# Moving the first batch's second Fourier transform behind the first value products

## The chip, the cores and the metric

The kernel runs on one core of a Trainium2 chip. The metric is the device time of one execution in microseconds (us). Three runs of the kernel before took 630.52, 630.96 and 631.91 us; their median is 630.96 us.

The engines named below are PE (TensorE, matrix products), DVE (VectorE), ACT (ScalarE), POOL (GpSimd) and SP (SyncE, which here only issues transfers). Each executes its own instructions strictly in the order in which they were written; between engines there are semaphore waits.

## The reference

The program computes attention with capped scores (cap 30), then a token mixer by a Fourier transform with a feed-forward layer, then a gated layer. Cut to the parts that matter here:

```python
# attention, 2 batches x 12 heads, 448 tokens, 64 channels a head
scores = cap * np.tanh(scale * (q @ k.T) / cap)
attn = softmax(scores); x = attn @ v            # -> (2, 448, 768)
# Fourier mixing and layer norm
X = np.fft.fft(np.fft.fft(x, axis=1), axis=2)
u = x + np.real(X)
un = (u - mean(u)) / np.sqrt(var(u) + 1e-6)     # over the 768 channels
u = u + np.maximum(un @ w_ch1, 0.0) @ w_ch2     # then the gated layer
```

## The kernel before

Everything is kept transposed: channels on partitions, 448 tokens along the free axis. The heads go two by two, so there are 12 pairs, numbered 0 to 11; pairs 0 to 5 are the first batch, 6 to 11 the second. A hand-written software pipeline (`loop`, lines 608 to 682) runs over the pairs and is inside `tc.manual_schedule()`: each engine does its work in exactly the written order.

One turn n of the loop does, in the order of PE:

- `values(n - 1, (0, 1))`, line 568: the first half of the value products (tile `o`) of the pair before;
- `scores(n, 3)`, line 542: the last score block of this pair (tile `s_3`);
- `turn(n + 1)`, line 511: the transposes of the next pair's keys and queries (tile `tr`);
- `values(n - 1, (2, 3))` and `totals(n - 1)`, lines 568, 579 and 581: the second half of `o`, and the softmax's denominators (tile `den`);
- `scores(n + 1, step)` for steps 0, 1, 2: the next pair's scores (tiles `s_0`, `s_1`, `s_2`).

ACT turns scores into tanh (line 547) and then exponentials (line 551). DVE makes the low halves of keys and queries (line 520), the reciprocals of the denominators (line 588) and the product with them (line 592). POOL adds up exponentials (lines 556 and 560).

The first batch is complete after pair 5. What follows for it, the Fourier transform and the layer norm, is put into the gaps of the second batch's pairs. A table named `others` (lines 982 to 1011) says at which place of which turn each piece stands. The places are, in the order of a turn: "loads", "values" (behind the first value products), "transposes" (behind `turn` and the last tanh), "halves", "values23" (behind the second value products), "halves" (behind the first exponentials, in spite of its name), "take", "divide", "score0" to "score2" (behind each step of the next scores). The pieces of this change are:

- `f.second(c)` for c = 0, 2, 4, line 252: the second stage of the transform for channel blocks c and c+1, eight matmuls into one tile `st`;
- `f.add(c)`, lines 259 to 262: four DVE instructions that add a block of `st` to x, in tile `xT`;
- `n0.total`, lines 272 to 275: DVE sums u over channel blocks into `acc_m`; `n0.mean`, line 286: one matmul, tile `mu`; `n0.centre`, line 291: two DVE instructions d = u - mu; `n0.square`, line 298: two ACT instructions; `n0.square_total`: DVE sums again, into `acc_v`; then `n0.variance` (lines 307 to 309), `n0.deviation` (lines 314 and 316) and `n0.row` (line 323) in turn 11;
- `part("w2_", i, ...)`: steps of the conversion of a weight block from 8-byte to 4-byte floats: 0 size (ACT, line 704), 1 clamp (709), 2 shift (712), 3 top (715), 4 bottom (718), 5 upper (721, on DVE for i = 0), 6 lower (724). Steps 1 to 4 and 6 are DVE's.

PSUM's tiles `s_*`, `tr`, `st` and `mu` share three buffers of two banks (`big_ps`, line 112; 3 of them by line 940). A new tile waits until the readers of the buffer's last tile are done. `o` and `den` have one buffer each.

After turn 12 comes a long stretch of matrix products (feed-forward, gated layer, output) in which PE works nearly without a gap.

Of the kernel before, what the change touches and what calls it, by code (L numbers as in the profile page):

```python
# [93 lines left out]
def attention_mixers_kernel(ctx, tc, bounded, q, k, v, cap, w_ch1, w_ch2, w_in, g_ln, w_sg, b_sg, w_out,  # L94
# [839 lines left out]
    with ExitStack() as fctx:  # L934
# [8 lines left out]
        with ExitStack() as actx:  # L943
# [8 lines left out]
            if bounded:  # L952
                f, n0 = fourier(0, fp, t2sb, POOL_FOLDS[0]), layer_norm(0, fp)
                f1, n1 = fourier(1, fp, t2sb), layer_norm(1, fp)
                raws, pieces = {}, {}
                do = functools.partial
# [6 lines left out]
                def convert(*key):  # L963
                    name, i = key
                    how = dict(raw=raws[key], pieces=pieces.setdefault(key, []))
                    if name == "w1_":
                        w1.append(columns(w_ch1, i, name, hi_copy=vec.tensor_copy, **how))
                    else:
                        w2.append(rows(w_ch2, i, name, hi_copy=None if i else vec.tensor_copy, **how))

                def part(name, i, *steps):

                    def go():
                        if (name, i) not in pieces:
                            convert(name, i)
                        for step in steps:
                            pieces[name, i][step]()

                    return go
# [18 lines left out]
                    (8, "transposes"): [do(f.first, 1, 3)],  # L998
                    (8, "halves"): [do(f.keep_first, 1), do(f.keep_first, 3), part("w1_", 3, 5, 6), do(f.reverse, 0),
                                    do(f.reverse, 1), part("w2_", 0, 1, 2, 3)],  # L1000
                    (8, "take"): [do(f.second, 0), do(f.add, 0), do(f.add, 1)], (8, "score2"): [part("w2_", 0, 4)],
                    (9, "transposes"): [do(f.second, 2)],
                    (9, "halves"): [do(f.add, 2), do(f.add, 3), part("w2_", 0, 5, 6)],
                    (9, "divide"): [do(f.second, 4)],
                    (9, "score1"): [do(f.add, 4), do(f.add, 5)], (9, "score2"): [n0.total, part("w2_", 1, 0, 1, 2)],
                    (10, "loads"): [do(get, "w2_", 2)],
                    (10, "transposes"): [n0.mean], (10, "halves"): [n0.centre],
                    (10, "take"): [n0.square, n0.square_total],
                    (11, "loads"): [do(f1.table, kind) for kind in (0, 2, 1, 3)],
                    (11, "transposes"): [n0.variance, n0.deviation, None], (11, "values23"): [n0.row],  # L1010
                }
# [2 lines left out]
            else:  # L1014
                load, prepare, score, flip, values = attention(ap, mix)
# [264 lines left out]
```

## Time and profile before

| | us |
|---|---|
| median of 3 runs | 630.96 (630.52 to 631.91) |
| the profiled execution | 632.45 |
| span of the profiled execution | 630.7 |
| PE busy | 615.2 (98%) |
| DVE busy | 494.0 (78%) |
| ACT busy | 271.2 (43%) |
| POOL busy | 105.3 (17%) |

The profiled execution is one run under the profiler; its span goes from the first to the last recorded instruction, and 1.75 us lie around it. A timeline row gives the start in us from the span's beginning, the duration, the engine, the line, the operation and its tiles, and in brackets how long the engine was idle before it and which instruction ended that. Equal instructions in succession are one row with a count; a matmul on 32-bit floats has two records, so eight of them show as x16. Matmuls are pipelined: a row's duration holds the tail of its last one, and the difference of two starts is the time that PE needs.

The stretch of the change is from 94 to 135 us: the scores of pair 9 begin at 97.26 us, those of pair 10 at 112.82 us, those of pair 11 at 124.28 us.

### The profile page before, as it was taken

To read this page: it belongs to the slowest core of one execution; us is meant where nothing else is said; L and a number is where in the kernel's file an instruction comes from. 1 tells how busy PE (TensorE), PEld (TensorE's weight loads), DVE (VectorE), ACT (ScalarE), POOL (GpSimd) and SP (SyncE) were. 2 spreads that over 40 slices of the span, in tenths; PEclk is the share of its full clock that TensorE was granted. 3 is DMA by queue.
4 is the path that set the end of the run, shared out by engine and by line. 5 is a ranking of instruction groups with operands and counts; after the bars stand their busy time and mean duration, and the time that the engine had idled before them with its cause. 6 is when DMAs were issued, how large, how long until landed. Compare 5 with 4: busy or idle time off the path is not lost.

```text
span 630.7 us, 8755 instructions
## 1 busy us (share of the span) xinstructions
PE 615.2 (98%) x3378; PEld 529.7 (84%) x3378; DVE 494.0 (78%) x727; ACT 271.2 (43%) x371; POOL 105.3 (17%) x153
## 2 busy tenths in 40 slices
PE   7999999899999999999999999999999999999996
PEld 5555576559888999999999999999999999989985
DVE  1789999999985688989966893788389879897551
ACT  3999865672312244334503440442135245453221
POOL 1877795353000000000000000000000000100000
PEclk9999999999999999999999999999999999999998
DMA  6746523300400146444530522245035304100123
GB/s 160 194 103 161 164 67 79 133 1 1 151 1 16 51 150 207 153 151 151 168 133 8 193 101 101 76 128 195 3 107 184 111 2 150 51 1 1 30 73 78
DMA packets 70034, 62.84 MB, mean 100 GB/s; under 512 B 36256, under 2 KB 63712, under 8 KB 69984
## 3 DMA queue, kind: packets, MB, share of 16 engines
q1 hardware_dynamic: 69056, 61.97, 32.2%
q8 instruction: 28, 0.46, 0.3%
q10 hardware_dynamic: 928, 0.23, 0.2%
q14 instruction: 22, 0.18, 0.1%
HBM read 59.44 MB, written 2.75 MB: 99 GB/s over the span
## 4 chain that ended last, share of the span: by engine, by line
PE 91%; DVE 6%; ACT 1%; DMA 1%; issue 0%; POOLq 0%; POOL 0%; ACTq 0%; DVEq 0%
PE h L143 27%; PE c L143 27%; PE o L568 5%; PE v L143 5%; PE out L143 5%; PE u L143 5%; PE s L542 5%; PE sg L143 2%; PE st L231 2%; PE den L579 1%; PE den L581 1%; PE tr L511 1%; PE st L252 1%; DVE r L588 1%; PE idle L155 1%; PE xt L907 1%
## 5 line engine op out<-in xcount | busy, mean ns | idle before, releaser
L143 PE MATMUL h<-un,w 128*128 128x448 f32 x864 | 175.0, 363 | 0.5 <-DVE un L335 0.5
L143 PE MATMUL c<-h,w 128*128 128x448 f32 x864 | 174.8, 363 | 0.0
L143 PEld LDWEIGHTS h<-un,w 128*128 128x128 f32 x864 | 161.7, 187 | 12.7 <-DVE un L335 0.8
L143 PEld LDWEIGHTS c<-h,w 128*128 128x128 f32 x864 | 161.9, 188 | 11.5 <-issue 0.4
L767 DVE TENSOR_TENSOR xT<-xT,c 128x448 f32<-128x448 f32 x60 | 36.9, 616 | 35.7 <-PE c L143 35.7
L1225 POOL CAST x<-x 128x384 fp32r<-128x384 f32 x2 | 1.3, 672 | 324.8 <-ACT x L134 324.3
L547 ACT ACTIVATE e<-s,tanh_scale 128x896 f32<-128x896 f32 (+1 forms) x48 | 41.0, 933 | 16.1 <-PE s L542 15.9
L568 PE MATMUL o<-e,v 128*64 128x448 f32 x192 | 41.1, 551 | 0.0
L556 POOL TENSOR_TENSOR t<-e 128x224 f32<-128x224 f32 x48 | 39.6, 856 | 2.9 <-POOL mix L531 2.0
L560 POOL TENSOR_TENSOR t<-t,e 128x224 f32<-128x224 f32 x48 | 39.7, 858 | 0.0
L551 ACT ACTIVATE e<-e,cap_pos 128x1792 f32<-128x1792 f32 (+1 forms) x24 | 37.7, 1622 | 0.0
L758 ACT ACTIVATE h<-h 128x448 fp32r<-128x448 f32 x40 | 21.7, 543 | 27.4 <-DVE h L759 17.5
L588 DVE RECIPROCAL r<-den 128x448 f32<-128x448 f32 x11 | 32.4, 2947 | 1.1 <-PE den L581 1.0
L143 PE MATMUL out<-gated,wo 128*128 128x448 f32 x144 | 30.8, 367 | 0.0
L143 PEld LDWEIGHTS v<-wv,x 128*128 128x128 f32 x252 | 29.7, 188 | 0.1
L143 PE MATMUL v<-wv,x 128*128 128x256 f32 x252 | 29.7, 279 | 0.0
L143 PE MATMUL u<-x,wu 128*128 128x448 f32 x144 | 29.1, 362 | 0.0
L542 PE MATMUL s<-qT,kT 64*128 64x448 f32 x216 | 26.4, 379 | 2.3 <-DVE qT L520 1.2
L542 PEld LDWEIGHTS s<-qT,kT 64*128 64x128 f32 x216 | 19.2, 184 | 11.1 <-ACT e L551 4.2
L143 PEld LDWEIGHTS u<-x,wu 128*128 128x128 f32 x144 | 26.9, 188 | 1.8
L143 PEld LDWEIGHTS out<-gated,wo 128*128 128x128 f32 x144 | 26.4, 188 | 2.0 <-ACT gated L134 0.2
L568 PEld LDWEIGHTS o<-e,v 128*64 128x64 f32 x192 | 11.8, 136 | 17.7 <-issue 16.2
(383 smaller groups left out, 891.5 us busy)
## 6 DMA issues: line engine op xcount, KB each, us to landing
k<-in_k SPq DMA_DIRECT2D x24, 112.0 KB, 2.7
out<-res SPq DMA_DIRECT2D x12, 224.0 KB, 2.5
q<-in_q SPq DMA_DIRECT2D x22, 112.0 KB, 2.7
t<-dft_channels SPq DMA_DIRECT2D x8, 291.0 KB, 4.9
v<-in_v SPq DMA_DIRECT2D x24, 96.0 KB, 2.3
w_0raw<-in_moe_w_ch SPq DMA_DIRECT2D x2, 768.0 KB, 5.1
w_1raw<-in_moe_w_ch SPq DMA_DIRECT2D x2, 768.0 KB, 5.8
w_2raw<-in_moe_w_ch SPq DMA_DIRECT2D x2, 768.0 KB, 4.7
```

The lines of the kernel that those rows point to most:

```text
L143: pe.matmul(ps, lhs(i, a), rhs(i, b), start=start and m == 0, stop=stop and m == last)
L155: pe.matmul(ps[:, 0:2 * P], idle[:, 0:P], idle, start=True, stop=True)
L231: pe.matmul(ps[:HS, m * 256:m * 256 + NE], fold[:, i, m * HS:(m + 1) * HS], tab[:, i, :], start=i == 0, stop=i == 2)
L542: pe.matmul(ps[:, i, :S], t[lo:hi, x, at:at + P], qT[lo:hi, y, :], start=m == 0, stop=m == 2)
L547: act.activation(es[n][:, 2 * step:2 * step + nr], sums.pop((n, step))[:, :nr, :S], AF.Tanh, scale=tanh_scale)
L551: act.activation(part, part, AF.Exp, scale=cap_pos)
L556: pool.tensor_tensor(t[:, j, q], es[n][:, j, q], es[n][:, 2 + j, q], op=ALU.add)
L560: pool.tensor_tensor(ts[n][:, j, q], ts[n][:, j, q], es[n][:, 4 + j, q], op=ALU.add)
L568: pe.matmul(os[n][halfs[j], :S], vts[n % 3][:, j, i], es[n][:, 2 * i + j if i < 3 else 6], start=i == 0, stop=i == 3)
L588: vec.reciprocal(r, den[:, :S])
L758: act.activation(h[:, 0], ps[:, i, :S], AF.Relu)
L767: vec.tensor_tensor(u[:, c, :], u[:, c, :], ps[:, :S], op=ALU.add)
```

## The change

The three `f.second` calls of the first batch leave their places, and so do their adds, the mean's sum, the mean and several conversions:

- `f.second(0)` stood before the scores of pair 9 ((8, "take")) and now stands behind the first value products of pair 8 ((9, "values")). Its adds come behind the reciprocal of pair 7 on DVE.
- `f.second(4)` stood before the scores of pair 10 ((9, "divide")) and now stands behind the first value products of pair 9 ((10, "values")). Its adds and `n0.total` go to turn 10 with it.
- `n0.mean` stood behind the transposes of turn 10 and now stands behind the second value products of pair 9 ((10, "values23")).
- Steps 5 and 6 of weight block 0 (DVE) move from turn 9 to turn 10, ahead of `n0.centre`; step 4 moves from behind the scores of pair 9 to turn 9's "halves".
- Steps 0, 1, 2 of weight block 1 (ACT, DVE, DVE) move from the end of turn 9 to the end of turn 10, behind the squares on ACT.

```diff
-                    (8, "take"): [do(f.second, 0), do(f.add, 0), do(f.add, 1)], (8, "score2"): [part("w2_", 0, 4)],
-                    (9, "transposes"): [do(f.second, 2)],
-                    (9, "halves"): [do(f.add, 2), do(f.add, 3), part("w2_", 0, 5, 6)],
-                    (9, "divide"): [do(f.second, 4)],
-                    (9, "score1"): [do(f.add, 4), do(f.add, 5)], (9, "score2"): [n0.total, part("w2_", 1, 0, 1, 2)],
+                    (9, "values"): [do(f.second, 0)],
+                    (9, "transposes"): [do(f.add, 0), do(f.add, 1), do(f.second, 2)],
+                    (9, "halves"): [part("w2_", 0, 4), do(f.add, 2), do(f.add, 3)],
                     (10, "loads"): [do(get, "w2_", 2)],
-                    (10, "transposes"): [n0.mean], (10, "halves"): [n0.centre],
+                    (10, "values"): [do(f.second, 4), do(f.add, 4), do(f.add, 5), n0.total],
+                    (10, "values23"): [n0.mean],
+                    (10, "halves"): [part("w2_", 0, 5, 6), n0.centre],
                     (10, "take"): [n0.square, n0.square_total],
+                    (10, "score2"): [part("w2_", 1, 0, 1, 2)],
```

On PE, around the scores of pair 10 (`s`), before: `st_0_4` is the last second unit, `o` the value products of pair 9, `tr` the transposes for pair 11, `mu` the mean.

```order
L252 MATMUL st_0_4_1227<-t2sb,back_1_1094 128x226 x2
L542 MATMUL s_0_1236<-qT_1189,kT_1188 128x448 x6
L542 MATMUL s_1_1243<-qT_1189,kT_1188 128x448 x6
L542 MATMUL s_2_1258<-qT_1189,kT_1188 128x448 x6
L568 MATMUL o_1285<-e_1070,v_148 64x448 x4
L542 MATMUL s_3_1292<-qT_1189,mix_134 128x448 x3
L511 MATMUL tr_1297<-ident,k_1143 128x112 x4
L511 MATMUL tr_1297<-ident,q_1146 128x112 x4
L286 MATMUL mu_1307<-acc_m_1267,mean_w 128x448
L568 MATMUL o_1285<-e_1070,v_148 64x448 x4
```

The same place of PE in the changed kernel:

```order
L542 MATMUL s_2_1239<-qT_1188,kT_1187 128x448 x6
L568 MATMUL o_1256<-e_1070,v_148 64x448 x4
L252 MATMUL st_0_4_1261<-t2sb,back_0_1092 128x226 x2
L252 MATMUL st_0_4_1261<-t2sb,back_1_1094 128x226 x2
L252 MATMUL st_0_4_1261<-t2sb,back_0_1092 128x226 x2
L252 MATMUL st_0_4_1261<-t2sb,back_1_1094 128x226 x2
L542 MATMUL s_3_1285<-qT_1188,mix_134 128x448 x3
L511 MATMUL tr_1290<-ident,k_1125 128x112 x4
L511 MATMUL tr_1290<-ident,q_1128 128x112 x4
L568 MATMUL o_1256<-e_1070,v_148 64x448 x4
L286 MATMUL mu_1313<-acc_m_1280,mean_w 128x448
```

The last second unit has passed three score steps and half of the value products, and the mean has passed the other half.

On DVE, from the last add of channel block 5 to the centring, before: `half` and `acc_m` are the mean's sum, `w_1cvt` a conversion of block 1, `kT` and `qT` the low halves of pair 11, `d` the centred tokens.

```order
L262 TENSOR_TENSOR xT_105<-xT_105,st_0_4_1227 128x223
L272 TENSOR_TENSOR half_1265<-xT_105 128x3x448
L274 TENSOR_TENSOR acc_m_1267<-half_1265 128x448
L275 TENSOR_TENSOR acc_m_1267<-acc_m_1267,half_1265 128x448
L709 TENSOR_SCALAR w_1cvt<-w_1cvt 128x768
L712 TENSOR_SCALAR w_1cvt<-w_1cvt 128x768
L520 TENSOR_TENSOR kT_1309<-tr_1297,kT_1309 128x448
L520 TENSOR_TENSOR qT_1310<-tr_1297,qT_1310 128x448
L291 TENSOR_TENSOR d_0_1333<-xT_105,mu_1307 128x1344
L291 TENSOR_TENSOR d_1_1335<-xT_105,mu_1307 128x1344
```

The same stretch of DVE in the changed kernel:

```order
L262 TENSOR_TENSOR xT_105<-xT_105,st_0_4_1261 128x223
L272 TENSOR_TENSOR half_1278<-xT_105 128x3x448
L274 TENSOR_TENSOR acc_m_1280<-half_1278 128x448
L275 TENSOR_TENSOR acc_m_1280<-acc_m_1280,half_1278 128x448
L520 TENSOR_TENSOR kT_1300<-tr_1290,kT_1300 128x448
L520 TENSOR_TENSOR qT_1301<-tr_1290,qT_1301 128x448
L721 CAST w_0_1011<-w_0cvt 128x768
L724 TENSOR_TENSOR w_0_1011<-w_0cvt,w_0_1011 128x768
L291 TENSOR_TENSOR d_0_1328<-xT_105,mu_1313 128x1344
L291 TENSOR_TENSOR d_1_1330<-xT_105,mu_1313 128x1344
```

Two conversion steps left the place ahead of `kT`, and two others, of block 0, came in between `qT` and the centring.

On PE, the next pair's scores in the changed kernel, with what they wait for (PE_49 is PE's own semaphore, DVE_49 is DVE's):

```order
L542 MATMUL s_1_1349<-qT_1301,kT_1300 128x448 [waits PE_49]
L542 MATMUL s_1_1349<-qT_1301,kT_1300 128x448 x5
L542 MATMUL s_2_1356<-qT_1301,kT_1300 128x448 [waits DVE_49,PE_49]
L542 MATMUL s_2_1356<-qT_1301,kT_1300 128x448 x5
L568 MATMUL o_1380<-e_1193,v_149 64x448 [waits DMAHW4_49,Activation_49]
L568 MATMUL o_1380<-e_1193,v_149 64x448 [waits DMAHW7_49]
L568 MATMUL o_1380<-e_1193,v_149 64x448 x2
L542 MATMUL s_3_1387<-qT_1301,mix_135 128x448 [waits Activation_49,Pool_49]
```

In both kernels `s_2` of pair 11 takes the PSUM buffer of `mu`, so it waits for the second centring instruction; `s_3` takes the buffer of `s_0`, so it waits for that tile's tanh.

## Rows read from the trace of the kernel before

**Rows 1.** Busy time and share of the span of each engine, from the page.
```profile
PE 615.2 (98%) x3378; PEld 529.7 (84%) x3378; DVE 494.0 (78%) x727; ACT 271.2 (43%) x371; POOL 105.3 (17%) x153
```

**Rows 2.** PE's waits, whole span: total us, times, longest us.
```profile
PE mu L286 <- DVE acc_m L275: 1.7, 2, 1.2
...
PE s L542 <- ACT e L547: 1.1, 2, 0.6
PE st L252 <- ACT pq L235: 0.9, 1, 0.9
```

**Rows 3.** PE timeline, pairs 9 to 11: start, us, instructions, idle time before.
```profile
99.30 0.89 PE L542 MATMUL s<-qT,kT 64*128 64x448 f32 x6 [0.56 <-ACT e L547]
...
109.57 3.32 PE L252 MATMUL st<-t2sb,back 113*128 113x226 f32 x16
...
120.20 0.99 PE L286 MATMUL mu<-acc_m,mean_w 128*128 128x448 f32 x2 [1.25 <-DVE acc_m L275]
121.12 1.72 PE L568 MATMUL o<-e,v 128*64 128x448 f32 x8
...
124.28 2.09 PE L542 MATMUL s<-qT,kT 64*128 64x448 f32 x18
...
127.95 0.88 PE L542 MATMUL s<-qT,mix 128*128 128x448 f32 x3
128.68 1.48 PE L155 MATMUL var<-ident 128*128 128x256 bf16 x12
```

**Rows 4.** Chain of waits in order of time: start, us, what.
```profile
93.33 0.75 PE den L581 x4
94.08 3.25 PE st L252 x16
...
100.19 1.65 PE o L568 x8
101.84 0.81 PE s L542 x3
102.65 0.77 PE tr L511 x8
...
124.35 2.02 PE s L542 x18
```

**Rows 5.** DVE timeline: conversions, first add, mean's sum, halves, centring; columns as PE's.
```profile
108.91 0.92 DVE L721 CAST w<-w_0cvt 128x768 fp32r<-128x768 f32 x1
109.87 1.29 DVE L724 TENSOR_TENSOR w<-w_0cvt,w 128x768 fp32r<-128x768 f32 x1
...
114.68 0.38 DVE L259 TENSOR_TENSOR xT<-xT,st 128x225 f32<-128x225 f32 x1
...
117.18 1.56 DVE L272 TENSOR_TENSOR half<-xT 128x1344 f32<-128x1344 f32 x1
...
121.04 0.62 DVE L520 TENSOR_TENSOR kT<-tr,kT 128x448 fp32r<-128x448 f32 x1
...
122.10 3.01 DVE L291 TENSOR_TENSOR d<-xT,mu 128x1344 f32<-128x1344 f32 x2
...
158.44 0.95 DVE L724 TENSOR_TENSOR w<-w_1cvt,w 128x768 fp32r<-128x768 f32 x1
```

**Rows 6.** ACT timeline: conversion's first step, squares, tanh of pair 11.
```profile
108.64 0.94 ACT L704 ACTIVATE w_1cvt<-w_1raw 128x768 f32<-128x768 f32 x1
...
123.68 2.80 ACT L298 ACTIVATE sq<-d 128x1344 f32<-128x1344 f32 x2 [0.23 <-DVE d L291]
126.38 3.31 ACT L547 ACTIVATE e<-s,tanh_scale 128x896 f32<-128x896 f32 x4
```

**Rows 7.** PE timeline, the first matmuls after the start, on idle data.
```profile
3.29 5.30 PE L155 MATMUL idle<-ident 128*128 128x256 bf16 x24 [3.29 <-POOL ident masks.py:199]
```

**Rows 8.** Stretches at the end: length, busy us by engine (PE first), PEclk, DMA.
```profile
624.50:625.00 0.50, 0.16 (x2) 0.00 (x0) 0.00 (x0) 0.26 (x1) 0.00 (x0) 1.00 0.14 33
...
626.50:627.00 0.50, 0.00 (x0) 0.00 (x0) 0.00 (x0) 0.00 (x0) 0.00 (x0) 0.80 0.18 47
```

## The prediction

> **What bounds the kernel now.** I read the page's busy shares first: PE is busy 98% of the span [rows 1], and no other engine is above 78%. PE's work is the same in both kernels, instruction by instruction, so the time can change only by the time in which PE stands still, or by PE's rate. PE's list of waits over the whole span comes next [rows 2]. Few are left, and three lie in the stretch of the change: the scores of pairs 9 and 10 each wait for a tanh, 0.56 us and 0.55 us (1.1 us in two, one of them shown [rows 2, 3]), and the mean waits 1.25 us for its sum [rows 3]. Together 2.36 us: that is all that the change could win here. Then I read the timelines of PE, DVE and ACT from 94 to 135 us to see what each instruction would wait for in its new place, and the chain of waits for PE's durations between gaps [rows 4]. The reader is to see in the DVE rows that the mean's wait ends with a DVE chain (adds, sum), and that the next tile on PE's way depends on the centring that follows it [rows 5].
>
> **The change part by part.** PE's durations are those of the chain [rows 4]: a pair's scores 2.02 us, half of the value products 1.65, a second unit 3.25, the last score block 0.81, the transposes 0.77, the denominators twice 0.75.
>
> *First second unit behind the value products.* Both kernels have finished the denominators at 93.33 + 0.75 = 94.08 us. From there the new order on PE is scores 2.02, values 1.65, unit 3.25, last scores 0.81, transposes 0.77, unit 3.25, values 1.65, denominators 1.50, scores 2.02, values 1.65: 18.57 us, so the last unit begins at 112.65. Both waits for tanh go, 1.11 us, since `s_2` no longer has to take the buffer of `s_0` just written. What each of these pieces needs is there: keys, queries and exponentials are made at least 1 us earlier. I cost this part at -1.11 us.
>
> *Last second unit and its adds.* It begins at 112.65 instead of 109.57 [rows 3]. Before, its result lay waiting, since DVE still had two conversions and a reciprocal to do and began the adds at 114.68 [rows 5]. Now DVE has nothing left by then and stands idle until the unit has ended: 112.65 + 3.32 (the unit's row [rows 3]) + 0.05 = 116.0. The cover that the conversions gave is gone, and the adds come 1.3 us later.
>
> *Sum and mean.* From the first add to the mean on PE it took 120.20 - 114.68 = 5.52 us, eight adds and three sums with nothing between [rows 3, 5]. So the mean begins at 116.0 + 5.5 = 121.5. PE gets there at 112.65 + 3.25 + 0.81 + 0.77 + 1.65 = 119.1. It waits 2.4 us instead of 1.25, although half of the value products now fills the time ahead of it.
>
> *Conversions ahead of the centring.* The sum ends at 121.4. Behind it on DVE stand the low halves of pair 11, 122.10 - 121.04 = 1.06 us, then the two conversion steps of block 0, 0.96 us (start to start) and 1.29, and then the two centring instructions, 3.01 [rows 5]: 121.4 + 1.06 + 2.25 + 3.01 = 127.7. Before, the centring ended at 122.10 + 3.01 = 125.1. On PE come the mean 0.92 (120.20 to 121.12 [rows 3]), denominators 1.50, and two of three score steps, two thirds of 2.02: 121.5 + 0.92 + 1.50 + 1.35 = 125.3. Then `s_2` of pair 11 needs the mean's buffer, which the centring holds until 127.7. That is a new wait of 2.4 us; before, PE came at 124.28 + 1.35 = 125.6, after the buffer was free, and so had none. Behind `s_2` on PE stand the value products and everything else of the turn. The conversions' 2.25 us is measured beside POOL's additions; the same step took 0.95 us instead of 1.29 where POOL was idle [rows 5]. In the new place POOL begins its additions of pair 10 within these steps, so I take the larger value; two steps that are both 0.35 us faster would take 0.7 us from the sum.
>
> By the Trainium skill (SBUF — State Buffer, section "SBUF: two separate sides") VectorE and GpSimd share a port pair as an exclusive lock, and who comes second is blocked for the other's whole instruction. The trace has a smaller price, 0.34 us for such a step; a full block would lengthen the wait by the rest of a POOL addition, and the sum with it.
>
> *Squares, size step and tanh on ACT.* ACT began the tanh of pair 11 at 126.38, 1.27 us after the centring's end [rows 6]. The same squares now leave it free at 127.7 + 1.27 = 129.0. Then stands the size step of block 1, which before lay at 108.64 in idle time, 0.94 us, and now delays the tanh to 129.9. Four tanh took 3.31 us for seven score blocks [rows 6], so the first, with two blocks, takes 0.95: 130.9. That frees the buffer for `s_3`. PE is ready at 127.7 + 0.67 + 1.65 = 130.0, so it waits another 0.9 us; before, `s_3` began at 127.95 [rows 3]. The second tanh ends at 131.85, and the variance's tile begins then instead of at 128.68 [rows 3]: 3.2 us later. The size step could at best be hidden, 0.9 us less; it could not gain.
>
> *The rest.* DVE's clamp and shift of block 1 come behind the sum of squares, where DVE waits for the variance anyway; SP's transfers keep their order, and the buffer of weight block 2 is free about 1 us later than before, tens of us ahead of its use. Nothing for these. If that cover failed, the transfer would delay ACT's first step on it, in the stretch of the long products, not PE in the attention.
>
> *Sum.* Waits removed 0.56 + 0.55 + 1.25 = 2.36; waits added 2.4 + 2.4 + 0.9 + 0.1 = 5.8; difference 3.4. The comparison of starts (131.85 against 128.68) gives 3.2, which I take, since it doesn't add up rounded gaps. The profiled execution's 632.45 us becomes 635.65. The runs lie lower (median 630.96), and a shift by waits is the same there: 634.2 us.
>
> **The rivals.**
>
> *The clock falls in a new wait.* After the last matmul of the kernel, which ends at 624.66 (0.16 us into its stretch), the granted clock is at 1.00 and falls at about 626.8 to half, that is from 2.4 to 1.2 GHz: 0.80 is the mean of 0.3 us at full and 0.2 us at half [rows 8]. PE had then been idle for 2.1 us. The two new waits have 2.4 us each, and no gap between products before was over 1.25. Against it: PE works right ahead of and behind each, and at the end it had thinned out before. The price: at the start 24 matmuls on idle data took 5.30 us, 0.22 each [rows 7], the same instruction 0.12 in the variance's tile [rows 3], so PE ran at half rate for some 5.3 us and lost 2.65. After a fall in the mean's wait the next wait hides up to 2.4 of it; after a fall in the second, up to 0.9. That gives 634.4 to 636.9, middle 636.
>
> By the Trainium skill (TensorE: Matmul & The Clock Gate, "HAM oscillation — how this bites in real kernels") bursts of matmuls with idle time between them can lose the full clock at each gap. By that the fall is likelier than I take it; the trace agrees at its end, where the clock fell 2.1 us after the last product, and shows no case of a gap of 2.4 us between two products.
>
> *Given back later.* PE waits later in the span, 0.9 us for `pq` and 1.7 - 1.25 = 0.45 for the second batch's mean [rows 2]. If these waits end at times that do not move, they swallow 1.35: +1.85, 632.8 us. Against it: they end with DVE and ACT work that itself starts from the denominators of the last pairs, and so moves along.
>
> *The centring's wait doesn't come.* If DVE gets through halves, conversions and centring by 125.3, and the tanh behind the squares with it, only the longer mean's wait is left, 1.15 against the 1.11 that went: 631.0. For that DVE would have to do 6.3 us of work in 3.9; rows of the same instructions with POOL idle save 0.7.
>
> *Faster.* The mean's sum is ready when PE arrives, and no wait takes the place of the old ones: -2.36, 628.6 us. It decides at one point: the last unit's first add must start by 119.1 - 5.5 = 113.6 us, and the centring must end by 125.3. The unit itself would have to begin 2.4 us before 112.65, with 18.57 us of PE work ahead of it and no wait in that to take out.
>
> **How the numbers follow.** Forecast 634.2 us, chance 0.63, its own range 632.6 (conversions 0.7 faster and the size step hidden) to 635.0 (PE's waits as the sum of gaps, and some 0.6 for what the rows round). Clock 0.15; given back 0.10; no centring wait 0.08; faster 0.04. The range from 632.4 to 636.6 holds the forecast, "given back" and most of the clock case. About 0.2% (1.3 us) is what a measurement of this kernel can tell from no change. Slower by more: forecast, clock and given back, 0.63 + 0.15 + 0.10, less 0.03 for the low end = 0.85; within: 0.08 + 0.02 = 0.10; faster: 0.04 and what I can't see, 0.05.
>
> **What would show it.** In the profile of the changed kernel: no wait of scores of pairs 9 and 10 for a tanh; DVE idle some 3 us ahead of the adds of channel blocks 4 and 5; the mean on PE waiting for `acc_m` 2.4 us; `s_2` of pair 11 waiting for `d` (line 291) about 2.4 us, and `s_3` for a tanh about 0.9; the variance's tile at 131.9 us. PE's total of idle time grows by a good 3 us, and every later instruction stands that much later. It would be wrong if the mean found its sum ready, if `s_2` of pair 11 didn't wait, or if PE's matmuls in pair 11 were slower than in pair 10.

## The result, and the profile after

The changed kernel takes 634.77 us (median of 6 runs, 634.45 to 635.76), the kernel before beside it 631.08 (6 runs, 629.89 to 631.91). The ratio is 1.0058, 95% interval [1.0048, 1.0068]: slower by 3.7 us, give or take 0.6. Forecast were 634.2 and a range from 632.4 to 636.6. The profiled execution of the changed kernel took 634.45 us with a span of 632.6.

Busy times hardly move against [rows 1]. PE's own rises by 0.7 us for the same 3378 instructions; in a second profile of the changed kernel, shown below, it is 615.1.

```profile
PE 615.9 (97%) x3378; PEld 530.2 (84%) x3378; DVE 494.2 (78%) x727; ACT 270.8 (43%) x371; POOL 104.1 (16%) x153
```

PE's list of waits after the change (who waits for whom, total us, times, longest us), against [rows 2]:

```profile
PE mu L286 <- DVE acc_m L275: 2.9, 2, 2.5
...
PE st L252 <- ACT pq L235: 0.9, 1, 0.9
PE s L542 <- ACT e L547: 0.5, 1, 0.5
...
PE s L542 <- DVE d L291: 0.3, 1, 0.3
```

The mean's two waits have grown from 1.7 to 2.9. Scores wait once for a tanh instead of twice, and that one is a new one, in pair 11. The wait for the centring (`d`) that the prediction put at 2.4 us is there, but with 0.27 us. PE's timeline tells why (start, duration, instructions, idle time before and what ended it; against [rows 3]):

```profile
111.84 3.32 PE L252 MATMUL st<-t2sb,back 113*128 113x226 f32 x16
114.84 0.95 PE L542 MATMUL s<-qT,mix 128*128 128x448 f32 x3
...
116.49 1.72 PE L568 MATMUL o<-e,v 128*64 128x448 f32 x8
120.73 1.83 PE L286 MATMUL mu<-acc_m,mean_w 128*128 128x448 f32 x2 [2.52 <-DVE acc_m L275]
122.49 1.70 PE L579 MATMUL den<-e,ones 128*64 128x448 f32 x4
...
126.63 0.88 PE L542 MATMUL s<-qT,kT 64*128 64x448 f32 x6 [0.27 <-DVE d L291]
127.44 1.72 PE L568 MATMUL o<-e,v 128*64 128x448 f32 x8
129.71 0.85 PE L542 MATMUL s<-qT,mix 128*128 128x448 f32 x3 [0.55 <-ACT e L547]
130.51 1.47 PE L155 MATMUL var<-ident 128*128 128x256 bf16 x12
```

The mean is one matmul with two records; it took 0.99 us before and 1.83 now, and the denominators behind it are slow too. The windows over the same stretch (length, busy us of PE, PEld, DVE, ACT and POOL, then the granted clock) show the reason (in the windows left out the clock is 0.50 or 0.51):

```profile
120.00:120.50 0.50, 0.00 (x0) 0.00 (x0) 0.50 (x1) 0.50 (x2) 0.00 (x0) 1.00 0.00 0
120.50:121.00 0.50, 0.27 (x1) 0.30 (x2) 0.50 (x2) 0.48 (x2) 0.00 (x0) 0.58 0.00 0
...
124.00:124.50 0.50, 0.50 (x6) 0.14 (x2) 0.50 (x1) 0.00 (x0) 0.50 (x2) 1.00 0.00 0
```

PE's last product ended at 118.21. The clock fell from 2.4 to 1.2 GHz at about 120.6, just ahead of the mean, and came back at 124.0. On DVE (against [rows 5]):

```profile
115.20 0.39 DVE L259 TENSOR_TENSOR xT<-xT,st 128x225 f32<-128x225 f32 x1 [3.20 <-PE st L252]
...
121.57 0.67 DVE L721 CAST w<-w_0cvt 128x768 fp32r<-128x768 f32 x1
122.27 1.29 DVE L724 TENSOR_TENSOR w<-w_0cvt,w 128x768 fp32r<-128x768 f32 x1
123.48 3.00 DVE L291 TENSOR_TENSOR d<-xT,mu 128x1344 f32<-128x1344 f32 x2
```

DVE stood idle for 3.20 us ahead of the adds. Behind the sum it did halves, conversions and centring back to back, as forecast, and in the second profile below, where PE's clock was full in these 3 us, the centring began just as long after the sum. On ACT (against [rows 6]):

```profile
125.06 2.79 ACT L298 ACTIVATE sq<-d 128x1344 f32<-128x1344 f32 x2 [4.08 <-DVE d L291]
127.75 0.92 ACT L704 ACTIVATE w_1cvt<-w_1raw 128x768 f32<-128x768 f32 x1
128.58 3.30 ACT L547 ACTIVATE e<-s,tanh_scale 128x896 f32<-128x896 f32 x4
```

For all comparisons below I take one measure from each profile, called the stretch: from the first product behind the denominators of pair 7 (94.01 us before, 93.40 after) to the variance's tile. Before it is 128.68 - 94.01 = 34.67 us, after 130.51 - 93.40 = 37.11, so +2.44. The rest of the span, from the first feed-forward product on, is 490.44 us in both. The two spans differ by 1.9 us only because this execution of before reached the stretch 0.61 us later; in all profiles of the study that point lies between 92.80 and 94.01, and the rest behind the first feed-forward product between 489.5 and 490.6 us long. So the stretch tells more than a difference of spans.

One more profile of the changed kernel, expected thus:

> The changed kernel once more, for a second look at where the clock falls: theory A with a fall in the second of the two waits (as two experiments have it) gives the mean 0.99 us, a wait of about 1.9 us at the third score step of pair 11, value products of 3 us behind it, and the variance's tile 3.4 to 3.7 us later than before, counted from the scores of pair 9; with a fall in the first wait as in the first profile 2.4 us later. Theory B: the same number of us lost in both, since the fall is the loss.

It took 634.94 us, and its stretch is 38.01, +3.34. PE's timeline:

```profile
120.39 0.99 PE L286 MATMUL mu<-acc_m,mean_w 128*128 128x448 f32 x2 [2.53 <-DVE acc_m L275]
121.31 0.97 PE L579 MATMUL den<-e,ones 128*64 128x448 f32 x4
...
122.96 1.49 PE L542 MATMUL s<-qT,kT 64*128 64x448 f32 x12
126.30 1.30 PE L542 MATMUL s<-qT,kT 64*128 64x448 f32 x6 [1.85 <-DVE d L291]
127.53 2.90 PE L568 MATMUL o<-e,v 128*64 128x448 f32 x8
130.36 0.86 PE L542 MATMUL s<-qT,mix 128*128 128x448 f32 x3
131.07 1.49 PE L155 MATMUL var<-ident 128*128 128x256 bf16 x12
```

Here the mean and the denominators ran at full rate, the wait for the centring is 1.85 us, and the clock fell right behind that one, at about 126.5 us: the value products took 2.90 us. So the clock fell once in each of the two profiles, at one of the two waits, and not at the same one. The mean granted clock of its six runs is 0.994 to 0.996 in every one, 0.997 in the profile of before.

### The profile page after: what moved, and what is told of

It reads as the page before. It is cut to its first block, busy times and chain, and to the rows that moved or that the text cites. A ratio compares the mean times of both kernels' runs of the same rounds, so it can differ in the third digit from the quotient of the medians.

```text
span 632.6 us, 8757 instructions
## 1 busy us (share of the span) xinstructions
PE 615.9 (97%) x3378; PEld 530.2 (84%) x3378; DVE 494.2 (78%) x727; ACT 270.8 (43%) x371; POOL 104.1 (16%) x153
## 4 chain that ended last, share of the span: by engine, by line
PE 87%; DVE 9%; ACT 1%; issue 1%; DMA 1%; POOLq 0%; POOL 0%; DVEq 0%; ACTq 0%; SPq 0%
PE c L143 27%; PE h L143 25%; PE o L568 5%; PE v L143 5%; PE out L143 5%; PE u L143 5%; PE s L542 5%; PE sg L143 2%; PE st L252 2%; DVE r L588 1%; PE st L231 1%; PE tr L511 1%; PE den L581 1%; PE den L579 1%; DVE un L335 1%
## 5 line engine op out<-in xcount | busy, mean ns | idle before, releaser
L556 POOL TENSOR_TENSOR t<-e 128x224 f32<-128x224 f32 x48 | 41.1, 888 | 2.9 <-POOL mix L531 2.0
L560 POOL TENSOR_TENSOR t<-t,e 128x224 f32<-128x224 f32 x48 | 37.0, 802 | 0.0
```

What stands on the lines that cost most here:

```text
L556: pool.tensor_tensor(t[:, j, q], es[n][:, j, q], es[n][:, 2 + j, q], op=ALU.add)
L560: pool.tensor_tensor(ts[n][:, j, q], ts[n][:, j, q], es[n][:, 4 + j, q], op=ALU.add)
```

## The experiments

Two theories stood against each other. The chain: the last unit lies later on PE, so the adds, the sum, the centring and the squares come later, and PE waits for each in turn. The clock: PE loses by running at half rate after a gap. All ratios are against runs of the kernel before on the same chip; its medians were 631.08 to 631.54 us, so medians of different experiments are compared to about half a microsecond only.

**The first unit alone.** Against the kernel before, only the first unit, its adds and the conversion step in their way are moved:

```diff
-(8, "take"): [do(f.second, 0), do(f.add, 0), do(f.add, 1)], (8, "score2"): [part("w2_", 0, 4)],
-(9, "transposes"): [do(f.second, 2)],
-(9, "halves"): [do(f.add, 2), do(f.add, 3), part("w2_", 0, 5, 6)],
+(9, "values"): [do(f.second, 0)],
+(9, "transposes"): [do(f.add, 0), do(f.add, 1), do(f.second, 2)],
+(9, "halves"): [part("w2_", 0, 4), do(f.add, 2), do(f.add, 3), part("w2_", 0, 5, 6)],
```

> Only the first second-stage unit moves behind the value products; the last unit, the sum, the mean and the conversions stay where they were before the change. Theory A (the loss comes from the late adds of the last unit and the DVE and ACT chain behind them): the wait of pair 9's scores for a tanh, 0.56 us, is gone and nothing comes in its place: 0.5 us faster than before, about 630.6 us, mean waiting 1.25 us as before, clock never at half in the attention. Theory B (the loss comes from the clock, which falls in the mean's wait): the same, since the mean's wait is no longer than before. A rival to both, that moving the first unit is part of the loss: 635 us or some part of the 3.7 us.

630.27 us, ratio 0.9985 [0.9977, 0.9994]; the stretch is 33.78, -0.89. The wait for the tanh in pair 9 is gone, and that is nearly all of it. PE's timeline before, at the scores of pair 9 (the row between stands in [rows 3]):

```profile
97.26 1.48 PE L542 MATMUL s<-qT,kT 64*128 64x448 f32 x12
...
100.12 1.72 PE L568 MATMUL o<-e,v 128*64 128x448 f32 x8
```

and with the first unit moved:

```profile
92.90 2.09 PE L542 MATMUL s<-qT,kT 64*128 64x448 f32 x18
94.92 1.72 PE L568 MATMUL o<-e,v 128*64 128x448 f32 x8
96.57 3.32 PE L252 MATMUL st<-t2sb,pq 113*128 113x226 f32 x16
99.57 0.95 PE L542 MATMUL s<-qT,mix 128*128 128x448 f32 x3
```

From their start to the next product the scores took 100.12 - 97.26 = 2.86 us before and take 94.92 - 92.90 = 2.02 now. So the wait listed with 0.56 us cost 0.84: besides the idle time, the tail of the product ahead of it is no longer overlapped (1.48 instead of 1.35, two thirds of 2.02), and the products behind it took 0.82 from start to start instead of 0.67. The unit itself takes 3.00 us here against 3.25 [rows 4], but the last score block (0.07), the transposes (0.13) and the middle unit (0.08) behind it take that much longer. The mean's wait is 1.15 us instead of 1.25. This half of the change is a gain.

**The last unit alone.** In the changed kernel the first unit goes back ahead of pair 9's scores:

```diff
-(9, "values"): [do(f.second, 0)],
-(9, "transposes"): [do(f.add, 0), do(f.add, 1), do(f.second, 2)],
-(9, "halves"): [part("w2_", 0, 4), do(f.add, 2), do(f.add, 3)],
+(8, "take"): [do(f.second, 0), do(f.add, 0), do(f.add, 1)], (8, "score2"): [part("w2_", 0, 4)],
+(9, "transposes"): [do(f.second, 2)],
+(9, "halves"): [do(f.add, 2), do(f.add, 3)],
```

> Only the last unit, its adds, the sum, the mean and the conversions move; the first unit stays ahead of pair 9's scores. Theories A and B: the whole loss of the change and 0.5 us more, since the scores of pair 9 wait 0.56 us for a tanh again: 635.2 us; the mean waits 2.4 to 2.5 us and the clock falls in that wait. The rival, that the first unit's move is part of the loss: clearly less than 634.8 us.

635.45 us, ratio 1.0066 [1.0054, 1.0078]; stretch 38.83, +4.16. PE's timeline has both waits:

```profile
121.95 0.99 PE L286 MATMUL mu<-acc_m,mean_w 128*128 128x448 f32 x2 [2.52 <-DVE acc_m L275]
...
127.86 1.16 PE L542 MATMUL s<-qT,kT 64*128 64x448 f32 x6 [1.84 <-DVE d L291]
128.95 3.06 PE L568 MATMUL o<-e,v 128*64 128x448 f32 x8
```

It was expected that the clock falls in the mean's wait. It did not: the mean took 0.99 us, and the clock fell behind the wait for the centring. The loss lies wholly in this half. The two halves add up: -0.89 + 4.16 = +3.27, against +3.34 in the second profile of the changed kernel, which has the clock's fall in the same wait.

**The mean's wait filled.** Twenty small products on idle data go into the mean's tile ahead of it; the mean's matmul overwrites them.

```diff
+            if bounded and not b:
+                stream(t.mu, 20)
```

> The changed kernel with 20 products on idle data written into the mean's tile ahead of the mean, to fill PE's 2.5 us wait; they take 0.11 us each, 2.2 us in all. Theory A (DVE and ACT chain): the clock stays at full, the mean and the denominators take 0.99 and 0.92 us again instead of 1.83 and 1.70, PE comes to the third score step of pair 11 some 1.6 us sooner and waits there that much longer, about 1.9 us instead of 0.27: time as the changed kernel's, 634.8 us within 0.4. Theory B (the clock): the 1.6 us that half rate cost come back: 633.1 us.

634.62 us, ratio 1.0050 [1.0037, 1.0064]; stretch 38.02, +3.35. The mean now follows products directly and runs at full rate, but the wait for the centring is 1.91 us and the clock falls right behind it, against the expectation of a full clock. Nothing was won.

**Both waits filled.** In addition, 16 such products go ahead of pair 11's third score step, into the tile of the value products, which overwrite them:

```diff
+                        if (n, step) == (last - 1, 1):
+                            os[n] = own.tile([P, 512], F32, tag="o", bufs=1, name=f"o{n}")
+                            stream(os[n], 16)
```

> The changed kernel with both new waits of PE filled: 20 products on idle data ahead of the mean and 16 (1.8 us) ahead of the third score step of pair 11, written into tiles that the real products overwrite. The DVE and ACT chain is as in the changed kernel. Theory A (chain sets the time, the clock adds little): the clock stays at full, the value products behind the third score step take 1.72 us instead of 2.97, the fourth score block then waits 0.9 us for its tanh, and the time is 0.4 to 0.6 us under the changed kernel: 634.2 us, 1.005 of before. Theory B (the clock makes most of the loss): 2 us or more under it, 632.8 us or less.

634.35 us (633.84 to 636.03), ratio 1.0056 [1.0040, 1.0072]; stretch 37.12, +2.45. PE's timeline (lines shifted by two):

```profile
120.53 1.02 PE L288 MATMUL mu<-acc_m,mean_w 128*128 128x448 f32 x2 [0.15 <-DVE acc_m L275]
...
124.57 1.92 PE L155 MATMUL o<-ident 128*128 128x256 bf16 x16
126.54 0.88 PE L544 MATMUL s<-qT,kT 64*128 64x448 f32 x6
127.34 1.72 PE L570 MATMUL o<-e,v 128*64 128x448 f32 x8
129.61 0.85 PE L544 MATMUL s<-qT,mix 128*128 128x448 f32 x3 [0.55 <-ACT e L549]
```

No product runs at half rate, and the six runs have a mean clock of 0.997 to 0.999. The stretch still is 2.45 us longer than before, and the time is that of the changed kernel. So the clock isn't needed for the changed kernel's loss: the chain alone, with the conversions in it, costs 2.45. The run also gives the price of the clock. Against the second profile after, from `s_2` to the variance's tile: 130.42 - 126.54 = 3.88 us here, 131.07 - 126.30 = 4.77 there, so 0.9 us for a fall at the second wait. For a fall in the mean's wait it is nothing (+2.44 against +2.45), because PE only arrives later at a wait that would have held it anyway.

**The centring ahead of the conversions.**

```diff
-(10, "halves"): [part("w2_", 0, 5, 6), n0.centre],
+(10, "halves"): [n0.centre, part("w2_", 0, 5, 6)],
```

> The changed kernel with the two conversion steps of weight block 0 behind the centring on DVE instead of ahead of it. Theory A: the centring ends 1.9 us earlier, the squares and the tanh of pair 11 follow, the waits of its third and fourth score blocks (0.27 and 0.55 us) go as far as PE, at half rate for a while, doesn't set the pace itself: 0.8 us faster than the changed kernel, about 634.0 us; if the clock does not fall, up to 1.9 us faster. Theory B: no gain beyond 0.3 us, since PE's rate sets the pace: 634.5 us.

632.81 us (631.71 to 634.36), ratio 1.0024 [1.0014, 1.0035]; stretch 35.39, +0.72, in an execution without half clock. PE's timeline:

```profile
120.23 0.99 PE L286 MATMUL mu<-acc_m,mean_w 128*128 128x448 f32 x2 [2.52 <-DVE acc_m L275]
...
122.81 2.50 PE L542 MATMUL s<-qT,kT 64*128 64x448 f32 x18
125.23 1.72 PE L568 MATMUL o<-e,v 128*64 128x448 f32 x8
127.50 0.84 PE L542 MATMUL s<-qT,mix 128*128 128x448 f32 x3 [0.54 <-ACT e L547]
```

No wait for the centring is listed, but the scores' row took 0.4 us longer than in [rows 3]. The centring on DVE, and a window that begins inside the row, show why:

```profile
121.26 3.02 DVE L291 TENSOR_TENSOR d<-xT,mu 128x1344 f32<-128x1344 f32 x2
124.42 0.88 PE L542 MATMUL s<-qT,kT 64*128 64x448 f32 x6
```

The centring ends at 124.28 and `s_2` begins at 124.42, so a wait of some 0.4 us, start to start, is left there. The conversions ahead of the centring cost 37.12 - 35.39 = 1.7 us in traces at full clock, and 634.77 - 632.81 = 2.0 in medians. The clock wasn't full in every run of this kernel: the mean granted clock is 0.998 or 0.999 in four of the eleven (631.71 to 632.76 us) and 0.993 to 0.997 in the others (632.46 to 634.36).

**The size step back to idle time.** ACT's step 0 of block 1 alone goes back to turn 9:

```diff
+(9, "score2"): [part("w2_", 1, 0)],
-(10, "score2"): [part("w2_", 1, 0, 1, 2)],
+(10, "score2"): [part("w2_", 1, 1, 2)],
```

> The changed kernel with the size step of weight block 1 (ACT, 0.92 us) back at the end of turn 9, where ACT is idle, instead of between the squares and the tanh of pair 11. Theory A: the tanh comes 0.9 us earlier, so the fourth score block's wait goes and the variance's tile begins up to 0.9 us earlier, less where PE at half rate sets the pace or the sum of squares then comes last (0.4 us later than PE): 0.3 to 0.9 us under the changed kernel, 634.2 us. Theory B: none of it, 634.8 us.

634.72 us, ratio 1.0050 [1.0036, 1.0063]; stretch 38.01, +3.34, the same as the second profile after. A gain was expected, and none can be seen: the clock fell at the second wait, the value products took 2.76 us, and the wait for the tanh, which this step lengthens, was hidden behind them.

**All conversions out of the way.** Steps 5 and 6 of block 0 go into DVE's idle time ahead of the adds, and steps 0 to 2 of block 1 back to turn 9:

```diff
+(9, "score2"): [part("w2_", 1, 0, 1, 2)],
-(10, "values"): [do(f.second, 4), do(f.add, 4), do(f.add, 5), n0.total],
+(10, "values"): [do(f.second, 4), part("w2_", 0, 5, 6), do(f.add, 4), do(f.add, 5), n0.total],
-(10, "halves"): [part("w2_", 0, 5, 6), n0.centre],
+(10, "halves"): [n0.centre],
-(10, "score2"): [part("w2_", 1, 0, 1, 2)],
```

> The changed kernel with all conversions off the path: the two steps of weight block 0 go into DVE's idle time ahead of the last adds, the three steps of block 1 go back to the end of turn 9. The last unit, its adds, the sum and the mean stay late. Theory A: the mean still waits 2.5 us; the centring then ends some 2 us earlier than in the changed kernel, and the third and fourth score blocks of pair 11 wait no more than 0.4 us; the variance's tile begins 0.3 to 0.7 us later than before (34.67 us after the scores of pair 9 begin or, there, the unit ahead of them), the time is 631.9 us at before = 631.5, up to 1 us more where the clock falls in the mean's wait. Theory B (the clock in the mean's wait is the loss): no better than the kernel with the two conversion steps behind the centring, 632.8 us.

633.02 us, ratio 1.0024 [1.0007, 1.0041]; stretch 35.75, +1.08. What is left is the mean's wait, and the clock falls in it:

```profile
120.69 1.83 PE L286 MATMUL mu<-acc_m,mean_w 128*128 128x448 f32 x2 [2.54 <-DVE acc_m L275]
122.45 1.59 PE L579 MATMUL den<-e,ones 128*64 128x448 f32 x4
...
124.72 2.09 PE L542 MATMUL s<-qT,kT 64*128 64x448 f32 x18
```

Filling DVE's idle time with the conversions did not delay the adds' sum, so that idle time was free room. No wait follows on PE that could take the clock's price over. From the mean to the next pair's scores PE took 124.72 - 120.69 = 4.03 us, against 122.96 - 120.39 = 2.57 at full clock in the second profile after. These 1.46 us are more than the 1.08 that is left. So what is left of the loss here goes with the clock, and the time is near theory B's 632.8 us and over theory A's 631.5 to 632.5. Without the fall its stretch would, by an estimate from these rows, be 1.08 - 1.46 = -0.4 us against before, or a little more for waits that PE would then meet; no run shows it. By this estimate the loss at full clock is that of the conversions, not of the late unit as such.

**Only the mean's matmul later.** The first unit alone, as above, and in addition the mean goes behind the second value products, and block 1's clamp and shift behind the squares; the last unit and the sum stay as before:

```diff
-(9, "score1"): [do(f.add, 4), do(f.add, 5)], (9, "score2"): [n0.total, part("w2_", 1, 0, 1, 2)],
+(9, "score1"): [do(f.add, 4), do(f.add, 5)], (9, "score2"): [n0.total, part("w2_", 1, 0)],
-(10, "transposes"): [n0.mean], (10, "halves"): [n0.centre],
-(10, "take"): [n0.square, n0.square_total],
+(10, "values23"): [n0.mean], (10, "halves"): [n0.centre],
+(10, "take"): [n0.square, n0.square_total], (10, "score2"): [part("w2_", 1, 1, 2)],
```

> The first unit moved as in the change, the last unit, its adds and the sum left where they were before it; of the rest of the change only that is taken which fills waits: the mean behind the second value products, and the clamp and shift of weight block 1 behind the sum of squares. Theory A: the mean finds its sum ready (1.15 us of wait gone beside the 0.56 of pair 9's scores), the centring frees the mean's buffer 0.4 us after PE wants it: about 1.0 us faster than before the change beyond... that is, in sum 0.5 us faster than the kernel with only the first unit moved, 629.8 us at before = 631.3. Theory B: the same, with the clock at full throughout. If the centring's wait takes all of it: as with only the first unit moved, 630.3 us.

629.82 us, ratio 0.9975 [0.9965, 0.9985]; stretch 33.12, -1.55. The mean's matmul no longer waits. The tanh wait of pair 10 is left, 0.55 us, and at the centring some 0.4 us that no list names: the scores of pair 11 are a row of 2.49 us instead of 2.09, as expected.

**The last unit between two score steps.** From that kernel, the last unit moves behind the second score step of pair 10 instead of ahead of the first:

```diff
-(9, "divide"): [do(f.second, 4)],
-(9, "score1"): [do(f.add, 4), do(f.add, 5)], ...
+(9, "score1"): [do(f.second, 4), do(f.add, 4), do(f.add, 5)], ...
```

> The kernel with the first unit moved and the mean behind the second value products, with the last unit moved behind the second score step of pair 10 instead of ahead of the first, its adds and the sum right behind. Theory A: pair 10's third score step no longer takes the buffer of the first (0.55 us of wait gone), DVE's reciprocal and conversions ahead of the adds keep it as busy as before, the mean waits up to 0.5 us for its sum: 0 to 0.3 us faster than the kernel with the last unit ahead, which took 629.8 us. A rival: the mean's wait takes all of the 0.55: same time.

629.43 us, ratio 0.9972 [0.9959, 0.9986]; stretch 32.66, -2.01. PE's timeline:

```profile
110.13 3.32 PE L252 MATMUL st<-t2sb,back 113*128 113x226 f32 x16
113.38 0.88 PE L542 MATMUL s<-qT,kT 64*128 64x448 f32 x6
...
119.22 1.02 PE L286 MATMUL mu<-acc_m,mean_w 128*128 128x448 f32 x2
```

Neither pair 10's third score step nor the mean waits; the 0.4 us at the centring stay (a row of 2.49 us again). The unit begins 110.13 - 93.94 = 16.19 us into the stretch, 1.4 us later than in the kernel just before (107.79 - 93.03 = 14.76) and 2.2 earlier than in the changed kernel (111.84 - 93.40 = 18.44). This version beats both the kernel before and the changed one; from the kernel just before it is not told apart by its time, since the intervals overlap, but by its trace.

## Why the prediction was right

- **Waits that go.** Forecast 1.11 us of tanh waits in pairs 9 and 10: both gone. Their worth was set too low: start to start the two rows of scores fell from 2.86 and 2.85 us to 2.04 and 2.02. The forecast's comparison of starts holds this, its sum of gaps does not.
- **A term mis-sized: the units.** They were costed at 3.25 us each; in the new place the first takes 100.09 - 97.10 = 2.99 and the last 114.84 - 111.84 = 3.00. The forecast is 0.25 us too high for each, but what stands behind them takes nearly that much longer: the way to the last unit, with the first in it, took 111.84 - 93.40 = 18.44 us against 18.57. In the mean's start it makes 0.1 us.
- **Last unit, adds, mean.** Forecast: DVE idle some 3 us, the mean's wait 2.4. Measured: 3.20, and 2.52 and 2.53. The mean's start is 27.33 us into the stretch in both profiles; the forecast has 121.5 - 94.08 = 27.4.
- **A term mis-sized: the conversions.** Forecast 2.25 us ahead of the centring; start to start 123.48 - 121.57 = 1.91, since step 5 took 0.67 us instead of 0.92; step 6 took 1.29 as before. By the Trainium skill (SBUF — State Buffer, "SBUF: two separate sides") where DVE reads two inputs from SBUF and POOL reads SBUF too, whichever starts first holds the shared ports for its whole instruction, and the other is blocked. The trace agrees with it. Step 6 began at 122.27 inside an addition of POOL that ended at 122.74, and took 0.34 us more than with POOL idle (0.95 [rows 5], 0.96 with all conversions out of the way); the next addition took twice as long as one that met no such step (each in a window of its own):

```profile
122.70 1.37 POOL L556 TENSOR_TENSOR t<-e 128x224 f32<-128x224 f32 x1
124.03 0.66 POOL L556 TENSOR_TENSOR t<-e 128x224 f32<-128x224 f32 x1
```

So the 0.34 us that the forecast took from the row before is no smaller price than the rule's; it fits the rest of an addition already under way.
- **The wait for the centring.** Forecast 2.4 us; 0.27 and 1.85 in the two profiles. It comes as the forecast has it. Its size is cut by the shorter conversions (0.3), by PE's own rows, which the forecast took 0.3 too short from the mean's start to the end of `s_1` (122.96 + 1.49 - 120.39 = 4.06 against 3.8), and in the first profile by the half clock, under which PE gets there later; `s_2` itself begins 33.2 us into the stretch in both (126.63 - 93.40, 126.30 - 93.06).
- **Size step and `s_3`.** Forecast 0.9 us; 0.55 with the full clock behind the centring, and no wait where PE is at half rate. The kernel without this step on the way showed no gain: this term is nothing where the clock falls late.
- **The rest and "given back".** Nothing is given back: the wait for `pq` stays 0.9 us, the second batch's mean waits 2.9 - 2.52 = 0.4 as before, and the span behind is equal.
- **The clock.** It had a chance of 0.15 as a rival, and it came in both profiles of the changed kernel. That judgement failed. A fall in the mean's wait was to be hidden by the next wait, and is. A fall at the second was to cost 2.65 less 0.9, that is 1.75, and costs 0.9, half of it: the second profile has the full rate back after some 3.4 us (126.5 to 130.0 by its windows) instead of 5.3. With the fall came a sign that the prediction itself had named as one of being wrong, products in pair 11 slower than in pair 10 (value products 2.90 against 1.72 us). And PE's idle time grew by 1.2 us in the first profile and 2.5 in the second, not by a good 3, since at half rate PE counts as busy. The prediction's chain stands without the clock, by the run with both waits filled; what it says of PE's rate doesn't.
- **The sum.** Forecast +3.2; measured +2.44 or +3.34 in the stretch, +3.7 ± 0.6 in the medians. Counted from 94.08 us, the forecast has the mean at 27.4, `s_2` at 33.6 and the variance's tile at 37.8; measured are 27.3, 33.2 and 37.1, with the clock's fall at the second wait 38.0. So the terms were too large by 0.1 up to the mean, 0.3 for the conversions and 0.3 for the size step and `s_3`, and the clock's 0 to 0.9, for which the forecast itself had nothing, stands against them. Part of why the total fits is thus luck; the sign and the chain are not. That medians differ by some 0.4 more than the larger of the two stretches stays open, within the interval.

## What to carry to other kernels

Before moving a producer later to remove a short wait of its neighbour, follow its own consumers to the next instruction of the bounding engine: here tanh waits of 1.11 us went, and a chain of DVE and ACT work that had been covered made new or longer ones: the mean's 1.25 us became 3.3 to 4.4 with those for the centring and the new tanh. What is moved along with it for room (conversions ahead of the centring: 1.7 us) should fill the idle time ahead of the chain, not stand inside it. A tile that takes over a rotating buffer waits for the last reader of whatever lay there, so a place between two tiles of a series can be better than the place ahead of them: here the tanh wait of 0.55 us went. (The place behind them was tried only together with other moves.)

## What the runs showed of the hardware

- The clock fell to half in gaps between products of 1.84 to 2.54 us, or within 0.5 us of their end, with PE busy ahead of and behind them; before, no gap in this stretch was over 1.25 us, and the profile of before ran its stretch at full rate. In six profiles the mean's gap of 2.52 to 2.54 us was left open. The clock fell there in two (the first of the changed kernel, and all conversions out of the way) and stayed full in four (the second of the changed kernel, the last unit alone, the centring first, the size step back). In three of these four, and with the mean's wait filled, it then fell at the gap of 1.84 to 1.91 us ahead of `s_2`; the fourth had no such gap. So a gap of this size is a risk, not a certainty, and the shorter of the two was no safer. By the Trainium skill (TensorE: Matmul & The Clock Gate, "HAM oscillation — how this bites in real kernels") a kernel can lose the full clock at each wait between bursts of products; the waits of its example are longer, some 3 to 5 us. The runs agree on the fall, at shorter waits and not at every one, and show that a wait behind it can take the price over (0 against 0.9 us).
- The same unit of 8 products takes 3.00 us from its start to the next product between value products and a score block that uses all 128 rows of the array, and 3.25 ahead of score products with 64 rows (also in the fastest kernel: 113.38 - 110.13). But the middle unit, between transposes and value products that use all rows, takes 3.25 as well (105.01 - 101.76 in the first profile after), and the products behind a faster unit gave most of the 0.25 us back. What it is was not tried.
- A listed wait can cost more than its idle time: 0.56 us of it was worth 0.84 us from start to start. And a wait can hide in a row: the 0.4 us at the centring stand in no list.
